# Attention outputs turned by TensorE instead of DMA transposes, the last two batches through DRAM, with feature pairs side by side

## The chip, the cores and the metric

The kernel runs on one core of a Trainium2 chip. The metric is the device time of one execution in microseconds. The time before is the median of nine runs.

## What is computed

Windowed attention over 8 batches, 8 heads, 576 positions and head size 64, then a gated network without a nonlinearity. Heads 0 to 3 look back over 32 positions, heads 4 to 7 over 128 positions in steps of four.

```python
scores = np.matmul(q, k.transpose(0, 1, 3, 2)) / np.sqrt(64)
rel = pos[:, None] - pos[None, :]
plain = (rel >= 0) & (rel < 32)                      # heads 0..3
dilated = (rel >= 0) & (rel < 128) & (rel % 4 == 0)  # heads 4..7
attn = softmax(where(mask, scores, -1e9)) @ v
x = attn.transpose(0, 2, 1, 3).reshape(4608, 512)
out = ((x @ w1) * (x @ w2)) @ w3 @ w_out
```

## The kernel before, in words

Everything is in bf16 but the inputs, the outputs and the sums. `w3 @ w_out` is formed once on the chip (`wf_sb`), so each token needs two products up (512 to 1024) and one down (1024 to 512).

*Names of the work.* A planner (`Plan`) holds a list of tasks with an engine, an assumed duration, what they depend on and a priority, lays them out in time once, when the program is built, and issues them in that order; each engine then runs its own list strictly in order. `SHIFT` adds to the priorities task by task, so it decides the order on every queue. `ON_DVE` names the PSUM copies that VectorE makes and not ScalarE. PSUM has eight banks, which the planner hands out too.

For one batch b there are two halves of heads (u = 0 plain, u = 1 dilated) and two halves of positions; the four half-steps are b.0 and b.1 (u = 0), b.2 and b.3 (u = 1). The tasks are:

- L: loads. GpSimd issues all loads that round to bf16: `load_rows` (q, k), `load_v_plain`, `load_v_dil`, `load_w` (w1 and w2, in two halves of 512 columns, LW0 and LW1), `load_wo`, `load_w3`. SP issues two f32 loads of batch 0, which ScalarE rounds. At most about eight GpSimd loads are under way; the next waits for the landing of an early one.
- T: VectorE turns q and k in blocks of 32 x 32 words of two bf16 (`turn`), so that pairs of features come to lie side by side (`qts`, `kts`); `QUARTERS` cuts some turns of batch 0 in four.
- S, E, M: scores on TensorE (L466, an operand with a step of two elements), exponentials on ScalarE (L477), masks on VectorE (L485).
- V, R, N: values on TensorE (L508, a row of ones gives the denominators), reciprocals (L519) and normalisation (L522) on VectorE into `xo`: 96 positions by 768 (three blocks of 256 features).
- The turn of `xo` to features by positions, into `XT[u]`. For batches below `TURNED` (2) it is X, six transposes on TensorE (L536), and K, the copy out of PSUM (L544 on ScalarE, L546 on VectorE). For the other six batches it is XD, one DMA transpose that SP issues (L549).
- A and B: the products up for a unit k of 288 tokens (unit k needs batch k // 2: both plain half-steps and one dilated one) and two 128-column pieces f (L573, 8 matmuls of 288 columns, 4 chunks of the contraction in `ORDER`, the dilated ones first). CA is ScalarE's copy of A (L584), G the gate on VectorE (L588) into the ring `gt`. The first `PARTED` of unit 0 are cut into a part on the plain chunks (name with p) and a part on the dilated ones.
- W3T, W3M, W3D: w3 turned on VectorE (L651), multiplied with w_out (L659), copied to `wf_sb`.
- Y, CY, ST: the product down for 128 tokens (L599, 8 matmuls of 512 columns), the copy (L609) into one of five buffers, and the stores, which SP issues (L643). The last Y is cut into two column ranges, copied by VectorE (FIN, L632).
- fill: single matmuls on zeros (L704) where TensorE would idle before the first A.

SP's list holds the stores and the DMA transposes in the planner's order: a store that is not ready holds up the transposes behind it, and the other way round. TensorE's list ends with A and B of unit 15 and Y32 to Y35.

Of the kernel before, what the change touches and what calls it, by code (L numbers as in the profile page):

```python
# [32 lines left out]
QUARTERS = ('kn',)  # L33
SINGLE = 0
TURNED = 2
# [9 lines left out]
ON_DVE = ('K0.3', 'K1.1', 'VK0.1.1', 'VK1.0.1', 'W3D2', 'W3D4', 'W3D5')  # L45
GRP = 5
WHOLE = ("qn", "kn")
B0_LOADS = ()
HELD = 4
MASK_AT = 22.5  # L50
PARTED = 4
BAND_AT = 8.2
IDENT_AT = -2.5
BUSY = 10000
LEAD = 1.2
WC = (512, 512)
SLACK = (400, 800, 2500, 5000)
# [138 lines left out]
def kernel(  # L196
# [22 lines left out]
    ctx.enter_context(tc.manual_schedule())  # L219
    plan = Plan()  # L220

    const = ctx.enter_context(tc.tile_pool(name="const", bufs=1))
    ps_pool = ctx.enter_context(tc.tile_pool(name="ps", bufs=1, space=bass.MemoryType.PSUM))
    ps = ps_pool.tile([P, 8, 512], F32, name="ps")

    w1_sb = const.tile([P, DCH, d_ff], BF16, name="w1_sb")
    w2_sb = const.tile([P, DCH, d_ff], BF16, name="w2_sb")
    wo_sb = const.tile([P, KFF, d_model], BF16, name="wo_sb")
    wf_sb = const.tile([P, KFF, d_model], BF16, name="wf_sb")
    XT = [  # L230
        const.tile([P, B * BLK, 2, QB], BF16, name="XT0"),
        const.tile([P, B * BLK, 2, QB], BF16, name="XT1"),
    ]
    gt = const.tile([P, KFF, RING], BF16, name="gt")
    ident = const.tile([P, P], BF16, name="ident")
    mask = const.tile([P, 16, QB], BF16, name="mask")
    vps = [const.tile([P, 4, 6, PITCH], BF16, name=f"vp{i}") for i in range(2)]
    vds = [const.tile([P, 4, 3, 2 * PITCH], BF16, name=f"vd{i}") for i in range(2)]
    bias = const.tile([P, 7, QB], BF16, name="bias")
    ets = [const.tile([P, 4 * GRP * QB + 32], BF16, name=f"et{i}") for i in range(4)]  # L240
    kts = [const.tile([P, 2, PADK + S, 2], BF16, name=f"kt{i}") for i in range(2)]
    qts = [const.tile([P, 2, S, 2], BF16, name=f"qt{i}") for i in range(2)]
    vts = [const.tile([P, 1, PADK + S, 2], BF16, name=f"vt{i}") for i in range(1)]
    warm = const.tile([P, 256], BF16, name="warm")
    rows_sb = {
        (nm, i): const.tile([P, n, 18 * D], BF16, name=f"{nm}{i}")
        for nm, n in (("qn", 2), ("kn", 2), ("vn", 1))
        for i in range(2)
    }
    w3ns = [const.tile([P, 8, 256], BF16, name=f"w3n{i}") for i in range(4)]  # L250
    w3Ts = [const.tile([P, 4, P, 2], BF16, name=f"w3T{i}") for i in range(3)]
    rcps = [const.tile([P, 4, 3], F32, name=f"rcp{i}") for i in range(4)]
    xos = [const.tile([P, 12 * D], BF16, name=f"xo{i}") for i in range(4)]
    asbs = [const.tile([P, 2, UNIT], BF16, name=f"asb{i}") for i in range(3)]
    osbs = [const.tile([P, d_model], F32, name=f"osb{i}") for i in range(OSB)]

    def bank(n, dtype=F32):
        at = ps[:, plan.now.place or 0, :]
        return (at if dtype == F32 else at.bitcast(dtype))[:, 0:n]

    def load_rows(nm, src, b, us):
        flat = src[b].rearrange("(u h) s d -> u (h s d)", u=2)
        flat = flat.rearrange("u (p x) -> p u x", p=P)
# [52 lines left out]
    def load_w(dst, src, f):  # L318
        nc.gpsimd.dma_start(  # L319
            out=dst[:, :, f], in_=src[:, f].rearrange("(a p) f -> p a f", p=P)  # L320
        )
# [165 lines left out]
    class Step:  # L487
# [41 lines left out]
        def cols(self):  # L529
            m0 = self.b * BLK + 3 * self.hf  # L530
            return XT[self.u][:, m0 : m0 + 3, :, :].rearrange("p m g x -> p (m g x)")

        def back(self):
            self.x = bank(6 * QB, BF16)
            for i in range(6):
                nc.tensor.transpose(  # L536
                    out=self.x[:, i * QB : (i + 1) * QB],
                    in_=self.xo[0:QB, i * P : (i + 1) * P],
                    identity=ident[0:QB, 0:QB],
                )  # L540

        def keep(self, eng):
            if eng == "ACT":
                nc.scalar.copy(out=self.cols(), in_=self.x)  # L544
            else:
                nc.vector.tensor_copy(out=self.cols(), in_=self.x)  # L546

        def back_dma(self):
            nc.sync.dma_start_transpose(  # L549
                out=self.cols().rearrange("p (i x) -> p i x", i=6),  # L550
                in_=self.xo[0:QB, :],
            )

    held = {}

    def unit_cols(k, c):

        b, hf = k // 2, k % 2  # L560
        if c < 2:
            x = XT[0][:, b * BLK : (b + 1) * BLK, c, 48 * hf : 48 * hf + 48]
            return x.rearrange("p m (r t) -> p r m t", r=2)
        return XT[1][:, 3 * k : 3 * k + 3, c - 2, :]
# [150 lines left out]
    def load(name, issue, move, deps, fn, b=0):  # L715
        dma_n[0] += 1
        return add(name, "DMA", (issue, move), [], fn, dma_n[0], lat=SLACK[min(b, 3)], after=deps)
# [28 lines left out]
    def loads_w12(c):  # L746
        return [
            load(f"LW{c}.{i}", 800, 1400 if WC[c] == 256 else 5.1 * WC[c], [],
                 lambda d=d, s=s: load_w(d, s, cols[c]))
            for i, (d, s) in enumerate(((w1_sb, moe_w1), (w2_sb, moe_w2)))  # L750
        ]
# [23 lines left out]
    for x in FIRST_LOADS:  # L775
# [6 lines left out]
        elif x[0] == "3":  # L782
            ts = [
                load(f"LW3.{c}.{g}", 550, 680, [], lambda c=c, g=g: load_w3(c, g)) for g in range(4)
            ]
            lw3[2 * c] = lw3[2 * c + 1] = ts
        elif x[0] == "d":
            loads_vd(c)
        elif x[0] == "v" and DIRECT_V <= c:
            loads_v(c)  # L790
        else:
            loads_rows(x[0] + "n", c, (int(x[2]),) if x[2:] else None)

    FUSED, w3m = [], []
    for ft in lw3:
        i = len(w3m) % 3
        x = add(f"W3T{ft}", "DVE", 1150, lw3[ft], lambda f=ft, i=i: w3_turn(f, i), RANK["W"],
                lat=80, after=w3m[-3:-2])
        z = add(f"W3M{ft}", "PE", 1728, [x, lwo[0], lwo[1]], lambda f=ft, i=i: w3_mul(f, i), 7,
                slot=1)  # L800
        w3m.append(z)
        name = f"W3D{ft}"
        eng, dur = ("DVE", 688) if name in ON_DVE else ("ACT", 585)
        FUSED.append(add(name, eng, dur, [z], lambda f=ft, e=eng: w3_done(f, e), -1, lat=100))

    kept, paced = {}, []
# [26 lines left out]
    for b in range(B):  # L833
# [71 lines left out]
        while steps < 4 * B:  # L905
            bb, i = steps // 4, steps % 4
            u, hf = i // 2, i % 2
            mine = [(bb, u, 3 * hf + mm) for mm in range(3)]
            if any(x not in grp_of for x in mine):
                break  # L910
            steps += 1
            parts = [grp_of[x][1:3] for x in mine]
            st = Step(bb, u, hf, parts)
            n = f"{bb}.{i}"
            ms = {id(t): t for x in mine for t in grp_of[x][3]}
            vv = add(f"V{n}", "PE", 390, list(ms.values()) + vals[(bb, u, hf)], st.values,
                     bb - 99 + rank("V", b), slot=2)
            for x in mine:
                readers.setdefault(grp_of[x][0], []).append(vv)
            if (bb, i) == (0, 2) and LATE:  # L920
                for t in late:
                    t.after.append(vv)
                    t.deps.append(vv)
            rc = add(f"R{n}", "DVE", 240, [vv], st.recip, 10 * bb + rank("N", bb), lat=0,
                     after=prev["x"][i])
            ns = [add(f"N{n}", "DVE", 960, [vv, rc], st.norm, 10 * bb + rank("N", bb), lat=80)]
            if bb < TURNED:
                x = add("X" + n, "PE", 270, ns + [idt], st.back, bb - 99 + rank("X", bb), slot=1)
                name = f"K{n}"
                eng, dur = ("DVE", 460) if name in ON_DVE else ("ACT", 640)  # L930
                x = [
                    add(name, eng, dur, [x], lambda st=st, e=eng: st.keep(e),
                        10 * bb + rank("K", bb), lat=100)
                ]
            else:
                x = [add("XD" + n, "SP", 1700, ns, st.back_dma, 0, lat=1200)]
            kept.setdefault(bb, []).append(x)
            prev["x"][i] = x
            vdone.setdefault((bb, u), []).append(vv)
# [114 lines left out]
```

## Time and profile before

| what | value |
|---|---|
| median of 9 runs | 249.99 us |
| lowest and highest | 248.41 and 258.92 us |
| the profiled execution | 251.70 us |
| its span | 249.8 us |
| products up, L573 | 1024 matmuls, 134.8 us busy |
| products down, L599 | 63.3 us busy |
| transposes, L536 | 48 matmuls |
| DMA transposes, L549 | 24, median 5.2 us from issue to landing, at most 16.0 |
| packets of GpSimd's queue | 39040, 62.0% of the DMA engines' time |
| packets of SP's queue | 20656, 28.2% |

Busy time of a group counts each matmul from its start to its modelled end, so overlapping ones count twice: 32 products in a row take 3.92 us, though each is listed with 286 ns. How long TensorE works on something is read from starts. In lists of instructions in order of time, a bracket gives the idle time before an instruction and what ended it. TensorE has two queues in the profile, PE for matmuls and PEld for weight loads, and a wait may show on both.

### The profile page before, as it was taken

The page shows a single profiled execution, that of the slowest core. Times are in us where ns is not written, and L with a number is a line of the kernel's source. Part 1 is how long each engine was busy: PE and PEld are TensorE (multiplying, and loading weights), DVE is VectorE, ACT ScalarE, POOL GpSimd, SP SyncE. Part 2 cuts the span into 40 slices and gives each one's busy share as a digit, 9 for nine tenths or more (in the row PEclk, how much of TensorE's full clock was granted, in tenths as well). Part 3 has the DMA queues.
Part 4 walks back from the last instruction along what each step waited for, and adds up shares of the span by engine and source line. Part 5 has one row for each costly group of instructions (what it writes and reads, how often), then busy time and mean ns, then how long its engine had stood idle before and what let it go on. Part 6 is the DMA issues. An engine that isn't in the chain of part 4 may idle for free.

```text
span 249.8 us, 6255 instructions
## 1 busy us (share of the span) xinstructions
PE 238.9 (96%) x2639; PEld 164.4 (66%) x2664; DVE 157.8 (63%) x266; ACT 107.0 (43%) x142; POOL 61.8 (25%) x94
## 2 busy tenths in 40 slices
PE   7889999989999999988999999999999999999994
PEld 5667787535675577666766767677676666777752
DVE  4878996987988977765629998267273652232221
ACT  5764633125636362524336253444344443323320
POOL 7896254584610630240100324000000000000000
PEclk9999999999999999999999999999999999999999
DMA  7999999999999999999993098822323124121114
GB/s 227 198 202 194 199 210 197 195 175 174 213 226 180 196 191 221 114 137 218 164 132 87 5 150 159 141 66 54 82 44 93 45 68 96 52 67 45 42 44 127
DMA packets 59724, 33.90 MB, mean 136 GB/s; under 512 B 44336, under 2 KB 50736, under 8 KB 59696
## 3 DMA queue, kind: packets, MB, share of 16 engines
q0 software_dynamic: 39040, 19.34, 62.0%
q1 hardware_dynamic: 20656, 14.16, 28.2%
q8 instruction: 21, 0.34, 0.6%
q14 instruction: 7, 0.06, 0.1%
HBM read 39.85 MB, written 9.44 MB: 197 GB/s over the span
## 4 chain that ended last, share of the span: by engine, by line
PE 71%; DMA 19%; POOL 4%; DVE 2%; issue 2%; DVEq 0%; POOLq 0%
PE ps L573 38%; PE ps L599 22%; DMA w3n<-in_moe_w_dram 7%; DMA w_sb<-in_moe_w_dram 5%; DMA XT<-xo 4%; PE ps L659 4%; PE ps L508 3%; PE ps L466 3%; DMA vn<-in_v_dram 3%; POOL mask L378 2%; PE ps L616 1%; POOL w_sb L319 1%; POOL vp L298 0%; POOL w3n L333 0%; DVE kt L399 0%
## 5 line engine op out<-in xcount | busy, mean ns | idle before, releaser
L573 PE MATMUL ps<-XT,w_sb 128*128 128x288 bf16 x1024 | 134.8, 286 | 1.9 <-DMA XT<-xo 1.7
L573 PEld LDWEIGHTS <-w_sb 128*128 128x128 bf16 x1024 | 97.9, 98 | 31.3 <-DMA XT<-xo 2.0
L588 DVE TENSOR_TENSOR gt<-ps,asb 128x576 bf16<-128x576 f32 x64 | 48.0, 755 | 56.1 <-PE ps L573 54.5
L584 ACT CAST asb<-ps 128x576 bf16<-128x576 f32 x64 | 40.7, 638 | 62.2 <-PE ps L573 60.1
L599 PE MATMUL ps<-wf_sb,gt 128*128 128x512 bf16 x257 | 63.3, 379 | 1.3 <-issue 0.2
L599 PEld LDWEIGHTS <-gt 128*128 128x128 bf16 x280 | 26.9, 98 | 27.5
L609 ACT COPY osb<-ps 128x512 f32<-128x512 f32 x35 | 20.4, 585 | 50.3 <-PE ps L599 49.2
L477 ACT ACTIVATE et<-ps 128x1920 bf16<-128x1920 f32 (+2 forms) x21 | 34.2, 1635 | 9.3 <-PE ps L466 9.3
L522 DVE TENSOR_TENSOR xo<-ps,rcp 96x768 bf16<-96x768 f32 x32 | 29.9, 947 | 0.7
L309 POOL DMA_DIRECT2D vd<-in_v_dram x32 | 21.4, 677 | 27.1 <-PE ps L508 24.9
L415 DVE STREAM_TRANSPOSE qt<-qn 128x320 uint32<-128x320 uint32 (+1 forms) x32 | 21.9, 703 | 2.8 <-PE ps L466 1.6
L485 DVE TENSOR_TENSOR et<-et,mask 128x960 bf16<-128x960 bf16 (+1 forms) x34 | 20.6, 643 | 1.3 <-ACT et L477 1.3
L298 POOL DMA_DIRECT2D vp<-in_v_dram x7 | 8.3, 1186 | 32.3 <-PE ps L508 20.2
L508 PEld LDWEIGHTS <-et 128*128 128x128 bf16 x384 | 14.2, 98 | 2.2 <-DMA vd<-in_v_dram 0.4
L659 PE MATMUL ps<-wo_sb,w3T 128*128 128x512 bf16 x62 | 14.2, 380 | 1.1 <-DVE w3T L651 1.0
L415 DVE STREAM_TRANSPOSE kt<-kn 128x256 uint32<-128x256 uint32 (+3 forms) x18 | 11.2, 640 | 4.3 <-PE ps L573 4.2
L466 PEld LDWEIGHTS <-kt 32*128 32x128 bf16 x768 | 9.1, 92 | 6.0 <-issue 5.3
L519 DVE RECIPROCAL rcp<-ps 96x12 f32<-96x12 f32 x32 | 6.6, 213 | 10.1 <-PE ps L508 9.9
L466 PE MATMUL ps<-qt,kt 32*128 32x96 bf16 x768 | 12.1, 201 | 0.4 <-DVE kt L399 0.4
L333 POOL DMA_DIRECT2D w3n<-in_moe_w_dram x16 | 9.3, 585 | 11.4 <-DMA wo_sb<-in_moe_w_out_dram 4.1
L659 PEld LDWEIGHTS <-w3T 128*128 128x128 bf16 x64 | 6.0, 98 | 8.7 <-DVE w3T L651 2.0
L651 DVE STREAM_TRANSPOSE w3T<-w3n 128x512 uint32<-128x512 uint32 x8 | 8.5, 1079 | 3.3 <-issue 1.8
(54 smaller groups left out, 103.2 us busy)
## 6 DMA issues: line engine op xcount, KB each, us to landing
qn<-in_q_dram POOLq DMA_DIRECT2D x6, 576.0 KB, 12.0
kn<-in_k_dram POOLq DMA_DIRECT2D x6, 576.0 KB, 12.2
w_sb<-in_moe_w_dram POOLq DMA_DIRECT2D x4, 512.0 KB, 10.3
w3n<-in_moe_w_dram POOLq DMA_DIRECT2D x16, 128.0 KB, 8.8
vp<-in_v_dram POOLq DMA_DIRECT2D x7, 288.0 KB, 9.1
out_dram<-osb SPq DMA_DIRECT2D x8, 224.0 KB, 2.4
out_dram<-osb SPq DMA_DIRECT2D x7, 256.0 KB, 3.7
out_dram<-osb SPq DMA_DIRECT2D x8, 192.0 KB, 3.5
```

Source lines behind the costliest of these rows:

```text
L309: nc.gpsimd.dma_start(out=vds[b % 2][p0 : p0 + n, :, mu, 16 : 16 + 2 * D], in_=v_rows(b, 4, 4 * t0 + res, [[4 * D, n], [S * D, 4], [1, 2 * ...
L415: nc.vector.transpose(out=o, in_=i)
L466: nc.tensor.matmul(out=self.sp[:, g, QB * i : QB * i + QB], lhsT=kt[prt, u, QB * m : QB * m + P, c], rhs=qq, start=(c == 0 and not biased) ...
L477: nc.scalar.activation(out=ev, in_=self.sp[:, :, 0:x], func=ACT.Exp, scale=scale)
L485: nc.vector.tensor_tensor(out=ev, in0=ev, in1=mk, op=AL.mult)
L508: nc.tensor.matmul(out=self.o[:, g, mm, :], lhsT=grp.et[:, c0 : c0 + P], rhs=vv, start=True, stop=True,)
L522: nc.vector.tensor_tensor(out=self.xo[0:QB, :].rearrange("p (m g d) -> p g m d", m=3, g=4), in0=self.o[0:QB, :, :, self.val : self.val + D ...
L573: nc.tensor.matmul(out=o[:, i, :], lhsT={"a": w1_sb, "b": w2_sb}[key][:, c, f * P : (f + 1) * P], rhs=unit_cols(k, c), start=(first and j ...
L584: nc.scalar.copy(out=held[("s", k, fs[0])], in_=held[("a", k, fs[0])])
L588: nc.vector.tensor_tensor(out=gt[:, fs[0] : fs[-1] + 1, c0 : c0 + UNIT], in0=held[("b", k, fs[0])], in1=held[("s", k, fs[0])], op=AL.mult,)
L599: nc.tensor.matmul(out=y, lhsT=gt[:, f, c0 : c0 + P], rhs=wf_sb[:, f, :], start=(f == 0), stop=(f == KFF - 1),)
L659: nc.tensor.matmul(out=o, lhsT=w3Ts[i][:, g // 2, :, g % 2], rhs=wo_sb[:, g, :], start=(g == 0), stop=(g == KFF - 1),)
```

## The change

Half-steps of batches 0 to 5 (`TURNED` is 6) are turned by TensorE; the DMA transposes are gone. For batches 6 and 7 there are three new tasks. F: VectorE turns `xo` in blocks of 32 x 32 words into a buffer that w3 had before. XA: SP issues three plain writes of it to DRAM, in runs of 128 bytes. UB: SP issues four reads from DRAM into `XT`, in runs of 1152 bytes, once the writes have landed. Since the turn works on words of two bf16, two neighbouring features stay side by side: `XT` is laid out with the pair innermost, the products read it with a step of two elements, TensorE's transposes read `xo` with a step of two and the copies out of PSUM write with a step of two. The rows of w1 and w2 are taken in the matching order (feature 256 u + 2 p + c), for which each of their four loads is cut into two. `QUARTERS` names q as well as k; `PARTED` is 9, so all eight products of unit 0 are cut by chunks and not four; `ON_DVE` names other copies; and all of `SHIFT` is another list, so the order on every queue is another one.

TensorE's order changes as follows where the prediction speaks of it. W3M7 comes before W3M0 and not after it. The transposes of batches 2 to 5 stand between B3.2 and B9.0; X3.1 is followed by Y10, six products with two V steps, X3.3 and X4.0, and A6.0. From A9.2 on the order is that of before. In GpSimd's list the first halves of w2 and w1 (two issues each) stand ahead of the loads of batch 1. From SP's list the transposes are gone; XA and UB of batches 6 and 7 stand among the stores ST19 to ST28, the end of it being XA7.2, ST26, UB7.2, XA7.3, ST27, UB7.3, ST28.

```diff
--- before.py
+++ after.py
@@ -30,9 +30,9 @@
 BIASED = 1
 LATE = False
 OSB = 5
-QUARTERS = ('kn',)
+QUARTERS = ('qn', 'kn')
 SINGLE = 0
-TURNED = 2
+TURNED = 6
 DIRECT_V = 1
 ORDER = (2, 3, 0, 1)
 RES = (0, 2, 1, 3)
@@ -41,14 +41,14 @@
 WARM = 25
 FILL = 110
...
-ON_DVE = ('K0.3', 'K1.1', 'VK0.1.1', 'VK1.0.1', 'W3D2', 'W3D4', 'W3D5')
...
+ON_DVE = ('K0.2', 'K1.2', 'VK0.0.1', 'VK0.1.1', 'VK1.0.0', 'VK1.0.1', 'W3D4')
 GRP = 5
 WHOLE = ("qn", "kn")
 B0_LOADS = ()
 HELD = 4
 MASK_AT = 22.5
-PARTED = 4
+PARTED = 9
 BAND_AT = 8.2
 IDENT_AT = -2.5
 BUSY = 10000
@@ -228,8 +228,8 @@
     wo_sb = const.tile([P, KFF, d_model], BF16, name="wo_sb")
     wf_sb = const.tile([P, KFF, d_model], BF16, name="wf_sb")
     XT = [
-        const.tile([P, B * BLK, 2, QB], BF16, name="XT0"),
-        const.tile([P, B * BLK, 2, QB], BF16, name="XT1"),
+        const.tile([P, B * BLK, QB, 2], BF16, name="XT0"),
+        const.tile([P, B * BLK, QB, 2], BF16, name="XT1"),
     ]
     gt = const.tile([P, KFF, RING], BF16, name="gt")
     ident = const.tile([P, P], BF16, name="ident")
@@ -251,6 +251,8 @@
     w3Ts = [const.tile([P, 4, P, 2], BF16, name=f"w3T{i}") for i in range(3)]
     rcps = [const.tile([P, 4, 3], F32, name=f"rcp{i}") for i in range(4)]
     xos = [const.tile([P, 12 * D], BF16, name=f"xo{i}") for i in range(4)]
+    dram = ctx.enter_context(tc.tile_pool(name="dram", bufs=1, space=bass.MemoryType.DRAM))
+    drs = [dram.tile([32, 12, 2 * QB], BF16, name=f"dr{i}") for i in range(4)]
     asbs = [const.tile([P, 2, UNIT], BF16, name=f"asb{i}") for i in range(3)]
     osbs = [const.tile([P, d_model], F32, name=f"osb{i}") for i in range(OSB)]
 
@@ -316,9 +318,11 @@
         nc.vector.tensor_copy(out=vp[0:32, :, 1:6, 0:D], in_=vp[96:128, :, 0:5, 0:D])
 
     def load_w(dst, src, f):
-        nc.gpsimd.dma_start(
-            out=dst[:, :, f], in_=src[:, f].rearrange("(a p) f -> p a f", p=P)
-        )
+        for u in range(2):
+            nc.gpsimd.dma_start(
+                out=dst[:, 2 * u : 2 * u + 2, f],
+                in_=src[2 * P * u : 2 * P * u + 2 * P, f].rearrange("(p c) f -> p c f", c=2),
+            )
 
     def load_wo(c):
         g = slice(4 * c, 4 * c + 4)
@@ -528,28 +532,43 @@
 
         def cols(self):
             m0 = self.b * BLK + 3 * self.hf
-            return XT[self.u][:, m0 : m0 + 3, :, :].rearrange("p m g x -> p (m g x)")
+            return XT[self.u][:, m0 : m0 + 3, :, :]
 
         def back(self):
-            self.x = bank(6 * QB, BF16)
-            for i in range(6):
-                nc.tensor.transpose(
-                    out=self.x[:, i * QB : (i + 1) * QB],
-                    in_=self.xo[0:QB, i * P : (i + 1) * P],
-                    identity=ident[0:QB, 0:QB],
+            self.x = bank(6 * QB, BF16).rearrange("p (m c x) -> p m c x", m=3, c=2)
+            xo = self.xo[0:QB, :].rearrange("p (m f c) -> p m f c", m=3, c=2)
+            for m in range(3):
+                for c in range(2):
+                    nc.tensor.transpose(
+                        out=self.x[:, m, c, :], in_=xo[:, m, :, c], identity=ident[0:QB, 0:QB]
+                    )
+
+        def keep(self, eng):
+            o = self.cols().rearrange("p m x c -> p m c x")
+            if eng == "ACT":
+                nc.scalar.copy(out=o, in_=self.x)
+            else:
+                nc.vector.tensor_copy(out=o, in_=self.x)
+
+        def flip(self):
+            self.y = w3ns[2 * self.u + self.hf].rearrange("p a x -> p (a x)")[:, 0 : 12 * D]
+            i = self.xo[0:QB, :].bitcast(U32).rearrange("p (m g f) -> p g m f", m=3, g=4)
+            o = self.y[0:QB, :].bitcast(U32).rearrange("p (g m x) -> p g m x", m=3, g=4)
+            nc.vector.transpose(out=o, in_=i)
+
+        def out_of(self):
+            self.dr = drs[2 * self.u + self.hf]
+            for a in range(3):
+                nc.sync.dma_start(
+                    out=self.dr[:, :, 64 * a : 64 * a + 64],
+                    in_=self.y[32 * a : 32 * a + 32, :].rearrange("p (q x) -> p q x", q=12),
                 )
 
-        def keep(self, eng):
-            if eng == "ACT":
-                nc.scalar.copy(out=self.cols(), in_=self.x)
-            else:
-                nc.vector.tensor_copy(out=self.cols(), in_=self.x)
-
-        def back_dma(self):
-            nc.sync.dma_start_transpose(
-                out=self.cols().rearrange("p (i x) -> p i x", i=6),
-                in_=self.xo[0:QB, :],
-            )
+        def back_in(self):
+            o = self.cols().rearrange("p m x c -> p (m x c)")
+            i = self.dr.rearrange("j (g m) x -> j g (m x)", g=4)
+            for g in range(4):
+                nc.sync.dma_start(out=o[32 * g : 32 * g + 32, :], in_=i[:, g, :])
 
 
 
@@ -559,9 +578,9 @@
 
         b, hf = k // 2, k % 2
         if c < 2:
-            x = XT[0][:, b * BLK : (b + 1) * BLK, c, 48 * hf : 48 * hf + 48]
+            x = XT[0][:, b * BLK : (b + 1) * BLK, 48 * hf : 48 * hf + 48, c]
             return x.rearrange("p m (r t) -> p r m t", r=2)
-        return XT[1][:, 3 * k : 3 * k + 3, c - 2, :]
+        return XT[1][:, 3 * k : 3 * k + 3, :, c - 2]
 
     def up(k, fs, key, chunks=ORDER, first=True, last=True):
         if first:
@@ -745,7 +764,7 @@
 
     def loads_w12(c):
         return [
-            load(f"LW{c}.{i}", 800, 1400 if WC[c] == 256 else 5.1 * WC[c], [],
+            load(f"LW{c}.{i}", 1300, 1400 if WC[c] == 256 else 5.1 * WC[c], [],
                  lambda d=d, s=s: load_w(d, s, cols[c]))
             for i, (d, s) in enumerate(((w1_sb, moe_w1), (w2_sb, moe_w2)))
         ]
@@ -791,7 +810,7 @@
         else:
             loads_rows(x[0] + "n", c, (int(x[2]),) if x[2:] else None)
 
-    FUSED, w3m = [], []
+    FUSED, w3m, w3t = [], [], {}
     for ft in lw3:
         i = len(w3m) % 3
         x = add(f"W3T{ft}", "DVE", 1150, lw3[ft], lambda f=ft, i=i: w3_turn(f, i), RANK["W"],
@@ -799,6 +818,7 @@
         z = add(f"W3M{ft}", "PE", 1728, [x, lwo[0], lwo[1]], lambda f=ft, i=i: w3_mul(f, i), 7,
                 slot=1)
         w3m.append(z)
+        w3t[ft] = x
         name = f"W3D{ft}"
         eng, dur = ("DVE", 688) if name in ON_DVE else ("ACT", 585)
         FUSED.append(add(name, eng, dur, [z], lambda f=ft, e=eng: w3_done(f, e), -1, lat=100))
@@ -933,7 +953,10 @@
                         10 * bb + rank("K", bb), lat=100)
                 ]
             else:
-                x = [add("XD" + n, "SP", 1700, ns, st.back_dma, 0, lat=1200)]
+                x = add("F" + n, "DVE", 850, ns, st.flip, 10 * bb + rank("N", bb), lat=80,
+                        after=prev["x"][i] if bb > TURNED else [w3t[2 * i], w3t[2 * i + 1]])
+                x = add("XA" + n, "SP", 1350, [x], st.out_of, 0, lat=2000)
+                x = [add("UB" + n, "SP", 3800, [x], st.back_in, 0, lat=2000)]
             kept.setdefault(bb, []).append(x)
             prev["x"][i] = x
             vdone.setdefault((bb, u), []).append(vv)
```

## The prediction

> **What bounds the kernel now.** I read the page's busy shares first, then busy time by stages, then the list of who waited for whom, then the chain that ended last, and last TensorE's instructions in order of time where that chain leaves TensorE.
>
> ```profile
> PE 238.9 (96%) x2639; PEld 164.4 (66%) x2664; DVE 157.8 (63%) x266; ACT 107.0 (43%) x142; POOL 61.8 (25%) x94
> ```
> ```profile
> 0.00:18.16 18.16, 15.23 (x241) 11.42 (x242) 12.59 (x42) 12.14 (x18) 15.69 (x29) 1.00 1.08 209
> 62.50:113.00 50.50, 48.53 (x554) 32.38 (x555) 40.42 (x66) 22.94 (x29) 14.63 (x20) 1.00 1.41 185
> 160.00:210.00 50.00, 49.58 (x588) 34.70 (x594) 26.21 (x42) 22.30 (x28) 0.00 (x0) 1.00 0.28 67
> ```
> The columns of the second view are length, busy PE, PEld, DVE, ACT and POOL, granted clock, DMA share, GB/s. TensorE is full in every stage after the first 18 us, at a granted clock of 1.00, while DMA is the crowded resource only before about 135 us. So the time is TensorE's work plus its few waits:
>
> ```profile
> PE ps L573 <- DMA XT<-xo: 1.7, 1, 1.7
> ...
> PE ps L659 <- DVE w3T L651: 1.0, 2, 0.8
> ...
> PE ps L536 <- DVE xo L522: 0.2, 1, 0.2
> PE ps L573 <- DMA w_sb<-in_moe_w_dram: 0.2, 1, 0.2
> ```
> ```profile
> 20.82 3.11 PE L573 MATMUL ps<-XT,w_sb 128*128 128x288 bf16 x24 [0.17 <-DMA w_sb<-in_moe_w_dram]
> ...
> 52.17 5.35 PE L659 MATMUL ps<-wo_sb,w3T 128*128 128x512 bf16 x24 [0.76 <-DVE w3T L651]
> ...
> 113.08 2.13 PE L573 MATMUL ps<-XT,w_sb 128*128 128x288 bf16 x16 [1.73 <-DMA XT<-xo]
> ```
> From 20.82 us to the end, the only waits of TensorE over 0.3 us are 0.76 us for the turned w3 and 1.73 us for a DMA transpose (A6.0, the first product of token unit 6, waits for XD3.2). The chain that ended last has the durations I use:
>
> ```profile
> 64.38 0.26 PE ps L536 x6
> ...
> 102.26 10.77 DMA XT<-xo
> ...
> 210.74 3.92 PE ps L573 x32
> ```
> Six transposes take 0.26 us of TensorE, 43 ns each. Thirty-two products take 3.92 us, 122.5 ns each. The late DMA transpose took 10.77 us from issue to landing, in a stage with a DMA share of 1.41.
>
> **The change, part by part.**
>
> *Sixteen half-steps (batches 2 to 5) go back to TensorE.* 16 x 0.26 = +4.16 us, in a stream that is full around all of them: all on the path. A page of the Trainium skill speaks against this harder: "TensorE: Matmul & The Clock Gate", Part 4, puts a transpose at about 275 ns in a kernel's context and says that it does not count as activity for the clock. By that page the sum would be 96 x 0.275 = 26 us. The trace has 43 ns for this very shape and no drop of the granted clock around them, so I take the trace.
>
> *Their evacuation.* 16 copies on ScalarE at 0.64 us (the row of L544, 638 to 646 ns) = 10.2 us. ScalarE is 22.9 of 50.5 us busy where most of them fall; its idle time hides them. Were that cover gone, each would delay a copy of A by 0.64 us. The copies now write every second element; the copy that already does so (L434, 768 elements, 802 ns) and the plain one (L544, 576 in 640 ns) lie on one line of 0.84 ns an element, so I add nothing. On VectorE one such copy of batch 0 (442 ns now) and one of batch 1 may lose speed, to at most 0.6 us by the same slope; +0.2 us each beside other work, nothing on the path.
>
> *The DMA transposes leave.* The 1.73 us wait goes: -1.73. Late next for A6.0 is the copy of X3.1 on ScalarE, whose transpose stands one Y (1.73 us) and six products (5.9 us) ahead of A6.0. Ends: -1.73, and 0 where that copy is late.
>
> *Waits for the new transposes.* Each stands in TensorE's fixed order behind a normalisation on VectorE (0.95 us); behind it stand products that need nothing from it, and they wait as well. Of the eight in the trace three made TensorE's two queues wait (0.8 us together), two of those in the start-up where nothing else was to do. Between 62.5 and 113 us VectorE is 80% busy. Ends: 0, and 16 x 0.4 = 6.4 us (0.4 is the longest such wait); I take +0.3, near the four of batch 1, which cost 0.2.
>
> *Start-up.* The weight loads are cut in two (four more GpSimd issues; the shortest plain load rows are 0.54 us, a whole weight load is 0.78, so up to 8 x 0.57 - 3.1 = +1.5 us on GpSimd's queue) and moved: the first halves of w2 and w1 now go ahead of the q and k loads of batch 1. The queue past them is GpSimd's: q, k and v of batch 1, then the second halves, then w3. In the trace w1's first half was issued at 5.67 and landed 8.1 us later (the shortest of the four weight loads), w2's at 11.02 with TensorE waiting to 20.82. The landings in between fit 190 to 195 GB/s of bf16 written. Counting bytes in the new order, both are there at about 17.7 us. The half-products A and B on XT0's chunks (eight instead of four) then start as soon as X0.1 is copied. Idle and fill-in matmuls between 16.86 and 20.82 are seven fills of 0.11 us and some 0.4 us of waits, 1.2 us in all: the most to gain. Ends: -1.2, and +2 if w1 (five issues further back) lands at 20 us. I take -0.6.
>
> *w3.* The program now runs W3M7 before W3M0, so the product that waited 0.76 us has 1.7 us more; as many bytes stand before its load as now. Ends: -1.0 (both waits go), and +1 from the four more issues. I take -0.76.
>
> *The last two batches.* Eight transposes on VectorE of 384 words (L415: 320 take 0.76, L399: 576 take 1.24; so 0.85 us) replace nothing on TensorE; VectorE is 26.2 of 50 us busy there. Then three writes to DRAM, a wait for their landing, and four reads, all in SP's order with stores behind them; ScalarE has five output buffers at about 6 us apart, which hides late stores. The tight place is A14.0. By the trace G12.6 ends at 206.2 and A14.0 runs at 218.2 (216.23 + 16 products). Flip to 207.1, three issues of 0.41 us (median of L643) to 208.3, landing after 1.6 to 3.8 us (stores) at 212 at the latest, four issues to 213.7, landing by 217.5: 0 us, with 0.7 us to spare at the slow end. A DMA transpose in this stretch took 2.5 to 5.2. Ends: 0, and +3 us if writing 128-byte runs is as slow as 5.2 us per leg. The skill's "DMA: Bandwidth & Descriptors", Specifications, says runs under 512 B are read, changed and written back. By that page the first leg is the slow one; no row here shows such a write.
>
> *Pairs next to each other.* The 1024 products now read their moving operand at a step of two elements. The only row with that step is the scores' (L466): 40 matmuls of 96 columns in 0.545 us, four at a time in different rows of the array, 54.5 ns per four. Half speed would be 80 ns for 96 columns, so that is out; at worst 54.5/96 = 0.57 ns a column against 0.425, which is 1024 x 288 x 0.143 ns = +42 us. At best 0. I take 0: the four start one after another, and 42.5 ns plus their offsets explains 54.5. Weights read with a step (L659) load in 98 ns like all others.
>
> **Sum.** 4.16 - 1.73 + 0.3 - 0.6 - 0.76 + 0 = +1.4 us. The profiled execution took 251.70 us (span 249.8 and 1.9 around it), so 253.1 by it. It stands 1.7 us above the median of 249.99, about what the wait for the DMA transpose cost. If the median run has that wait too, it becomes 251.4; if it has not, it becomes 253.1. The lowest run, 248.41, without that wait gives 248.41 + 3.1 = 251.5. I say **252.0**, 0.8% over the median: within what a measurement of this kernel can tell from no change, which is about 1%.
>
> **The rivals.**
> - *A14.0 waits for DRAM* (slower). Place: 207 to 218 us, SP's queue. Price: whatever the two legs take beyond 218.2; at 5.2 us a leg and 0.95 us an issue about 3 us, so 255. It decides from a landing 0.7 us later than I count. For it: the read waits behind the write's landing and a store. Against: stores land in 2.6 us at the median. Chance 0.13.
> - *TensorE waits at the new transposes* (slower). Price 16 x 0.25 = 4 us instead of 0.3: 255.7. For it: VectorE at 80%. Against: the four of batch 1 waited 0.2 us together. Chance 0.16.
> - *Start-up and w3 give all they can.* -1.2 and -1.0, no wait at a transpose: 249.99 + 4.16 - 1.73 - 2.2 = 250.2, down to 248.5 where the median run's wait was longer. To be faster by 1% the transposes would have to cost nothing as well. For it: the plain chunks of A and B can begin earlier. Against: bytes ahead of the second weight halves are the same. Chance 0.17.
> - *The step of two slows the products.* 260 to 292. Chance 0.03.
> - The forecast, 251 to 253.5: 0.51.
>
> **How the numbers follow.** The range leaves out the step's rival and the tails of the others: 249.0 (all savings) to 255.7 (one of the two waits in full). Faster by over 1% is under 247.5: 0.08, half of the third rival. Slower by over 1% is over 252.5: both slow rivals, the step's, and a fifth of the forecast, 0.42. Within 1%: 0.50.
>
> **What would show it.** Right: 144 transposes at L536's successor, 0.26 us for each six; products still at 3.92 us for 32; no TensorE wait for XT near 111 us; the turned-w3 wait below 0.3 us; the first product of A at or before 18 us; no wait ahead of A14.0. Wrong: products over 123 ns, a granted clock under 1.00, waits of the transposes for xo of over 1 us in sum, TensorE waiting for DMA into XT after 205 us, or w1 landing after 20 us.

## The result, and the profile after

The changed kernel takes 259.5 us (median of 21 runs, 258.63 to 260.51), the kernel before 250.66 us (63 runs, 248.31 to 262.64). The ratio is 1.0385, with a 95% interval of 1.0363 to 1.0408: 3.9% slower, 3.8 us above the upper end of the range. Executions of a kernel that are disturbed (those of before up to 262.64 us, and the one that was profiled of b1_mask below, in which one DMA transpose is waited for 5.86 us) are left out of the comparisons, so a ratio is not always the quotient of the two medians.

The profiled execution of after has a span of 258.0 us, against 249.8: 8.2 us to account for. The busy shares say only that TensorE is still what bounds the kernel, with 97 instructions more (96 of them the new transposes):

```profile
PE 246.5 (96%) x2736; PEld 167.1 (65%) x2762; DVE 163.9 (64%) x275; ACT 119.8 (46%) x159; POOL 64.5 (25%) x98
```

Two events cut both executions into the same three pieces: the first product of w3 with w_out, and the first Y. First before, then after; the columns are those of the stages shown ahead (length, busy PE, PEld, DVE, ACT, POOL, granted clock, DMA share, GB/s):

```profile
0.00:46.07 46.07, 42.74 (x575) 33.02 (x575) 35.76 (x77) 24.64 (x34) 29.29 (x50) 1.00 1.26 203
46.07:62.49 16.42, 15.56 (x154) 7.34 (x157) 13.36 (x18) 4.93 (x7) 10.14 (x14) 1.00 1.58 182
62.49:249.80 187.31, 180.60 (x1917) 124.07 (x1936) 108.65 (x173) 77.42 (x102) 22.32 (x30) 1.00 0.76 115
```
```profile
0.00:50.51 50.51, 44.24 (x576) 33.41 (x577) 37.87 (x80) 24.72 (x33) 34.44 (x59) 1.00 1.22 195
50.51:66.21 15.70, 15.55 (x156) 7.51 (x157) 12.37 (x16) 6.29 (x9) 7.78 (x11) 1.00 1.57 190
66.21:258.00 191.79, 186.72 (x2006) 126.22 (x2028) 113.67 (x180) 88.80 (x118) 22.26 (x30) 1.00 0.58 104
```

| stage | change |
|---|---|
| start-up, to the first w3 product | 50.51 - 46.07 = +4.44 us |
| w3 stage | 15.70 - 16.42 = -0.72 us |
| first Y to the end | 191.79 - 187.31 = +4.48 us |

The reader is to see that TensorE's idle time grew by 2.9 us in the start-up (3.3 to 6.3, the length less the busy PE) and fell by 1.6 in the last stage (6.7 to 5.1), where the extra time is busy time. These are two different losses. The first shows in TensorE's instructions of after in order of time:

```profile
16.73 0.47 PE L512 MATMUL ps<-vd,et 128*128 128x65 bf16 x10 [1.15 <-DMA vd<-in_v_dram]
...
33.83 0.20 PE L512 MATMUL ps<-vp,et 128*128 128x65 bf16 x1 [1.49 <-DVE et L489]
34.91 0.49 PE L512 MATMUL ps<-vp,et 128*128 128x65 bf16 x11 [0.87 <-DVE vp L318]
...
37.30 0.43 PE L542 MATMUL ps<-ident,xo 96*128 96x96 bf16 x6 [0.53 <-DVE xo L526]
```

These waits make 4.04 us, and none of them is for a weight. (Before has waits of its own in this piece, 0.25, 0.22, 0.17 and 0.24 us among them.) The three after 33 us have one origin. The mask multiplication L489 is VectorE's, and the same view of VectorE names what it waited for:

```profile
33.11 1.23 DVE L489 TENSOR_TENSOR et<-et,mask 128x960 bf16<-128x960 bf16 x2 [3.97 <-POOL mask L382]
34.37 0.48 DVE L318 COPY vp<-vp 32x1280 bf16<-32x1280 bf16 x1
```

VectorE stood for 3.97 us; the halo copy of `vp` (L318) and the normalisation behind it in its list came late with it. GpSimd's list of after shows why the last mask was so late:

```profile
26.16 0.71 POOL L322 DMA_DIRECT2D w_sb<-in_moe_w_dram  x1 [0.67 <-DMA qn<-in_q_dram]
...
28.19 0.59 POOL L337 DMA_DIRECT2D w3n<-in_moe_w_dram  x1 [0.71 <-DMA w_sb<-in_moe_w_dram]
29.89 0.58 POOL L337 DMA_DIRECT2D w3n<-in_moe_w_dram  x1 [1.11 <-DMA w_sb<-in_moe_w_dram]
31.64 0.70 POOL L268 DMA_DIRECT2D qn<-in_q_dram  x1 [1.18 <-ACT asb L603]
32.38 0.70 POOL L382 TENSOR_SCALAR mask<-bias 128x192 bf16<-128x192 bf16 x1
```

The mask (task masks1) needs 0.70 us of GpSimd and nothing from these loads. But it stands behind two loads of w3 and one of q, and each of those waits for an earlier load to land before GpSimd issues it. (For the q load the bracket names a copy by ScalarE, which this load does not need. The load of `vp` issued at 19.46 us took 11.6 us and landed at 31.1, just ahead of it.) In before it stood ahead of them:

```profile
21.77 0.71 POOL L378 TENSOR_SCALAR mask<-bias 128x192 bf16<-128x192 bf16 x1
```

The second loss is in the products. The last 48 products in a row, first before, then after:

```profile
233.17 6.04 PE L573 MATMUL ps<-XT,w_sb 128*128 128x288 bf16 x48
```
```profile
241.05 6.20 PE L592 MATMUL ps<-XT,w_sb 128*128 128x288 bf16 x48
```

0.16 us over 48 products is 3.3 ns each. The Y behind them, whose operands are laid out as before, did not change: 23 of their matmuls take 5.34 us in both traces. With b6's 2.6 ns a product (below) the account of the last stage reads 4.16 (transposes) - 1.73 (the wait that went) + 832 x 2.6 ns = 2.2: +4.6 against +4.48 measured. The start-up is explained less closely. Idle time grew by 2.9 us, the 192 products there make 192 x 2.6 ns = 0.5, and the 25 warm-up matmuls at its start took 5.52 us instead of 5.00; that is 3.9 of the 4.44 us. The last 0.5 us is not taken apart.

### The profile page after: what moved, and what is told of

It reads as the page before. It is cut to its first block, busy times and chain, and to the rows that moved or that the text cites. A ratio compares the mean times of both kernels' runs of the same rounds, so it can differ in the third digit from the quotient of the medians.

```text
span 258.0 us, 6508 instructions
## 1 busy us (share of the span) xinstructions
PE 246.5 (96%) x2736; PEld 167.1 (65%) x2762; DVE 163.9 (64%) x275; ACT 119.8 (46%) x159; POOL 64.5 (25%) x98
## 4 chain that ended last, share of the span: by engine, by line
PE 84%; DMA 8%; POOL 3%; issue 2%; DVE 2%; POOLq 0%; DVEq 0%
PE ps L592 46%; PE ps L618 23%; DMA w_sb<-in_moe_w_dram 8%; PE ps L678 5%; PE ps L512 4%; PE ps L470 3%; PE ps L542 2%; DVE et L489 1%; POOL vd L311 1%; PE ps L635 1%; POOL mask L382 1%; POOL w_sb L322 1%; DVE xo L526 0%; POOL qn L268 0%; POOL vn L268 0%
## 5 line engine op out<-in xcount | busy, mean ns | idle before, releaser
L592 PE MATMUL ps<-XT,w_sb 128*128 128x288 bf16 x1024 | 137.8, 286 | 0.2 <-DMA w_sb<-in_moe_w_dram 0.2
L592 PEld LDWEIGHTS <-w_sb 128*128 128x128 bf16 x1024 | 95.6, 96 | 32.9 <-DMA w_sb<-in_moe_w_dram 0.5
L489 DVE TENSOR_TENSOR et<-et,mask 128x960 bf16<-128x960 bf16 (+1 forms) x34 | 20.7, 647 | 6.4 <-POOL mask L382 4.0
L419 DVE STREAM_TRANSPOSE qt<-qn 128x320 uint32<-128x320 uint32 (+3 forms) x34 | 22.1, 673 | 3.9 <-PE ps L470 2.6
L549 ACT COPY XT<-ps 128x576 bf16<-128x576 bf16 x22 | 17.8, 810 | 12.3 <-PE ps L542 12.3
```

The costliest lines, as they stand in the source:

```text
L419: nc.vector.transpose(out=o, in_=i)
L489: nc.vector.tensor_tensor(out=ev, in0=ev, in1=mk, op=AL.mult)
L592: nc.tensor.matmul(out=o[:, i, :], lhsT={"a": w1_sb, "b": w2_sb}[key][:, c, f * P : (f + 1) * P], rhs=unit_cols(k, c), start=(first and j ...
```

## The experiments

Theory 1: the step of two in the products' moving operand costs 2 to 3 ns each, some 3 us in all. Theory 2: the start-up lost about 3 us because the last mask stands late in GpSimd's list; its rival 2a: the cut of the weight loads into eight issues is what costs, wherever the mask stands. Theory 3: the 2.5 us of gains that the prediction counted are real for every execution; its rival: they were waits of the profiled execution only. Where not said otherwise, ratios are to before, spans are those of profiled executions.

**a1_rows: pairs only where the turn by VectorE needs them.** Edit of after:

```diff
-        const.tile([P, B * BLK, QB, 2], BF16, name="XT0"),
+        const.tile([P, TURNED * BLK, 2, QB], BF16, name="XT0"),
...
+        const.tile([P, (B - TURNED) * BLK, QB, 2], BF16, name="XP0"),
```

> The changed kernel with the feature pairs side by side only for batches 6 and 7; for batches 0 to 5 the features lie in two rows as before, so the products of units 0 to 11 read with a step of one and the copies out of PSUM write with a step of one. The order on every queue is that of the changed kernel. Theory 1 (a step of two slows the products): 32 products of units 0 to 11 take 3.92 us again, those of units 12 to 15 keep 4.01; 768 x 3 ns = 2.3 us less span, about 255.7, and the copies on ScalarE fall from 0.81 to 0.64 us without an effect of their own. Rival (the 4.01 us come from something else of the new kernel, for instance its other order): no stretch of products changes, span 258.0.

Ratio 1.0335 (1.0284 to 1.0385), median 257.74 us, span 255.4. That is 2.6 us below after by the spans and 1.8 by the medians. One execution now holds both kinds of product, and that decides. TensorE in order of time (each length runs to the modelled end of the last product, so 4.08 here is 3.92 us from start to start):

```profile
132.47 4.08 PE L605 MATMUL ps<-XT,w_sb 128*128 128x288 bf16 x32
...
215.44 4.16 PE L605 MATMUL ps<-XP,w_sb 128*128 128x288 bf16 x32
```

0.08 us over 32 products is 2.5 ns each, at the same granted clock (1.00 around both). From the first Y to the end, where 576 products read XT, the time fell from 191.8 to 190.5 us: -1.3, for 576 x 2.6 ns = 1.5. Theory 1 holds. The rest of the 2.6 us is not this theory's: the wait for `vd` was 0.65 us shorter, and the start-up has a loss of its own, told at the end.

**a2_mask: after with the last mask further up.** Edit:

```diff
+    order.remove(by['masks1'])
+    order.insert(order.index(by['masks4']) + 1, by['masks1'])
```

> The changed kernel with one instruction moved: the last mask on GpSimd (192 columns) stands right after the mask of its list that came third, ahead of the loads it stood behind; nothing else moves. Theory 2 (the start-up loses its time to this mask, which stands behind loads that wait for landings): VectorE's wait of 4.0 us for the mask goes, and with it TensorE's 1.5 and 0.9 us at L512 and the 0.5 us at L542; span shorter by 2.4 to 2.9 us, about 255.4. Rival (the second weight halves and the v load of batch 1 are late as well): another wait takes the place within 1 us of it, span shorter by less than 1 us.

Ratio 1.0285 (1.0245 to 1.0325), median 256.66, span 254.9: 3.1 us below after, for moving an instruction of 0.7 us. TensorE's waits over 0.5 us, but for the fills (columns: us in total, times, longest):

```profile
PE ps L512 <- DMA vd<-in_v_dram: 1.0, 1, 1.0
PE ps L470 <- DVE kt L403: 0.6, 1, 0.6
PE ps L678 <- DVE w3T L670: 0.6, 1, 0.6
```

The waits for `et`, `vp` and `xo` are all gone, and the first w3 product starts at 46.77 instead of 50.51 us. 0.6 of the 3.7 us is given back behind it: w3's last loads are issued only 0.5 to 0.9 us earlier than in after (from 46.92 instead of 47.81 us on), so the turned w3 is late next.

**a3_whole: after with each weight load in one issue again, the mask left where it was.** The rows of w1 and w2 are then in the order of before; the products' number, shapes and steps are those of after. Edit:

```diff
     def load_w(dst, src, f):
-        for u in range(2):
-            nc.gpsimd.dma_start(
-                out=dst[:, 2 * u : 2 * u + 2, f],
...
+        nc.gpsimd.dma_start(
+            out=dst[:, :, f], in_=src[:, f].rearrange("(a p) f -> p a f", p=P)
+        )
```

> The changed kernel with each load of w1 and w2 as one issue again, in the row order of before (so the features meet other rows of the weights and the output is not the reference's); the order on every queue stays. Theory 2a (the cut of the loads delays the queue behind them): the last mask runs about 1.5 us or more earlier than 32.4, and TensorE's wait at L512 shrinks by as much; span 256 to 257. Rival 2b (its place in the list delays the mask, not the cut): the mask still runs after 31 us, span within 0.7 us of 258.0.

Ratio 1.0281 (1.0241 to 1.0322), median 256.54, span 254.9: the same 3.1 us. GpSimd in order of time:

```profile
28.51 0.71 POOL L268 DMA_DIRECT2D qn<-in_q_dram  x1 [2.48 <-DMA w_sb<-in_moe_w_dram]
29.24 0.70 POOL L380 TENSOR_SCALAR mask<-bias 128x192 bf16<-128x192 bf16 x1
```

With four issues less, the mask in the same place of the list runs at 29.24 instead of 32.38 us, and no wait for `et` is left. So in this order the cut matters as much as the place, and rival 2a cannot be put aside yet.

**b2_split: before with the weight loads cut in two, nothing else.** Edit of before, with the rows in their old order:

```diff
     def load_w(dst, src, f):
+        for u in range(2):
...
+                in_=src[2 * P * u : 2 * P * u + 2 * P, f].rearrange("(a p) f -> p a f", p=P),
```

> The kernel before with each load of w1 and w2 cut into two issues, same rows, same order on the queues. Theory 2b (the cut costs little, GpSimd's queue waits for landings anyway): within 0.7 us of before. Rival 2a (four more issues and the limit on loads under way push w3 and the masks back): 1.5 us or more, with a longer wait for the turned w3 at 52 us.

Ratio 1.0005 (0.9961 to 1.0049), span 247.6. The cut alone costs nothing: its mask still starts at 25.39 us, early enough. Rival 2a falls as a cause by itself.

**b1_mask: before with the mask late, loads whole.** One load of w3 moves with it. Edit of before:

```diff
+    order.remove(by['LW3.2.3'])
+    order.insert(order.index(by['A0.4']) + 1, by['LW3.2.3'])
+    order.remove(by['masks1'])
+    order.insert(order.index(by['LW3.2.3']) + 1, by['masks1'])
```

> The kernel before with the last mask on GpSimd moved behind the load of q of batch 2 and two loads of w3, as it stands in the changed kernel; one of these loads is issued at 31.05 us in the trace of before, so the mask would end at about 32.4 instead of 22.5. Theory 2 (the place of the mask is what the start-up lost): VectorE's first masking waits from 28.5 to 32.4 us, TensorE waits at L508 for 2 to 3 us, and the whole span grows by that, to about 252.3. Rival (the start-up of the changed kernel lost by its loads): less than 1 us.

Ratio 1.024 (1.0181 to 1.0299), median 255.6. The mask now starts at 31.56 us. The place alone, pushed this far, costs before 2.4%, about 6 us: more than expected. The wait at the V steps is there (TensorE's waits), and the stage behind it shows what came on top; the long wait for a DMA transpose in this execution lies at 121 us, far behind both:

```profile
PE ps L508 <- DVE et L485: 3.0, 2, 2.7
```
```profile
34.00:37.70 3.70, 3.70 (x28) 2.61 (x27) 2.91 (x6) 0.64 (x1) 1.73 (x4) 0.55 1.23 208
```

After the wait TensorE ran 3.7 us at a granted clock of 0.55, which costs 3.7 x 0.45 = 1.7 us more. In this execution the first w3 product starts 4.6 us late: 3.0 + 1.7. What the remaining 1 to 2 us of the ratio are is open.

So theory 2 holds in this form: cut and place together make the mask late, and undoing either of them gives the 3.1 us back.

**a4_twice: after with the transposes of batches 2 to 5 done twice.** Edit:

```diff
-            for m in range(3):
+            for m in 2 * (0, 1, 2) if self.b >= 2 else range(3):
```

> The changed kernel with the transposes of batches 2 to 5 done twice by TensorE, 96 matmuls more, the same output. Theory (each six cost 0.26 us of a full stream): 16 x 0.26 = 4.2 us more, span 262.2. Rival (they sit in idle time of TensorE, and the loss is elsewhere): less than 1 us more.

Ratio 1.0571 (1.0526 to 1.0616), median 263.77, span 262.1: +4.1 us over after, for 96 more transposes at 43 ns (4.13). All of them lie on the path.

**b3_w3, b4_x32, b5_both: before with the counted gains alone.** b3 swaps W3M7 and W3M0 (with their turns and copies). b4 turns half-step 3.2, the one that made A6.0 wait, by TensorE after Y9 and drops XD3.2; b5 does both.

```diff
+    for x, y in (("W3T0", "W3T7"), ("W3M0", "W3M7"), ("W3D0", "W3D7")):
+        i, j = order.index(by[x]), order.index(by[y])
+        order[i], order[j] = order[j], order[i]
...
+    x = Task("X3.2", "PE", 0, [], st.back, 0, 1, 0, ())
+    order.insert(at, x)
...
+    order.remove(by["XD3.2"])
```

> The kernel before with W3M7 ahead of W3M0 (and the turns and copies that belong to them swapped), as in the changed kernel; nothing else. Theory: the wait of 0.76 us for the turned w3 goes, 0.5 to 0.8 us less. Rival: the load of the next piece lands late as well, no gain.

> The kernel before with one of its 24 DMA transposes (half-step 3.2, the one that TensorE waited 1.73 us for) done by TensorE, six matmuls after Y9, and copied by ScalarE. Theory: 0.26 us more work and 1.73 us less wait, 1.0 to 1.5 us less in the profile. Rival (another transpose is late in its place, or the wait is there only in some executions): less than 0.5 us.

> The kernel before with W3M7 ahead of W3M0 and half-step 3.2 turned by TensorE, the two parts of the new order that removed waits. Theory: no wait for the turned w3 and none for the DMA transpose of 3.2; 0 to 0.4% less than before, since most executions of before have neither wait in full. Rival: another transpose becomes late and takes the gain back.

Ratios 0.997 (0.9919 to 1.0022), 1.0012 (0.9967 to 1.0056) and 0.9976 (0.9938 to 1.0014). In b3's profile the wait for w3T is gone, in b4's and b5's the wait for XT; the time does not follow. Nor is it shown that the edits removed them. b2, which keeps the order of w3 and the DMA transpose of 3.2, has neither wait in its profile: TensorE runs without a gap through the w3 products, and through A6.0, the second 16 of these 32:

```profile
46.58 10.54 PE L661 MATMUL ps<-wo_sb,w3T 128*128 128x512 bf16 x48
...
108.82 4.08 PE L575 MATMUL ps<-XT,w_sb 128*128 128x288 bf16 x32
```

b4 has one in the start-up instead, where its edit changes nothing:

```profile
PE ps L573 <- ACT asb L584: 0.7, 1, 0.7
```

So of the 2.5 us that two waits of one profiled execution promised, at most 0.6% (1.5 us) can be in a comparable execution of before, and nothing is shown. How long TensorE waits for the DMA transpose of 3.2 differs from profile to profile: not at all in b2 and b3, 1.2 us in b6, 1.7 in before, 5.9 in b1. All 18 executions of b4 and b5, which turn 3.2 by TensorE, lie between 248.54 and 250.76 us, those of before on the same two chips between 248.21 and 258.80. That suggests that this one transpose spreads them; it is not shown. No kernel tried here beats before measurably.

**b6_step: before with products that read every second element.** The buffer is filled as before and read with the step. Edit of before:

```diff
+        x = XT[1][:, 3 * k : 3 * k + 3, :, :].rearrange("p m g x -> p m (g x)")
+        return x[:, :, c - 2 : 192 : 2]
```

> The kernel before with the products reading every second element of the same two-row buffer (so they mix features and positions, and the output is not the reference's); all else as before. Theory 1: 32 products take 4.0 us instead of 3.92, 1024 x 3 ns = 3 us more, 1.2% over before on the same chip. Rival: the products stay at 3.92 us, and the slower ones of the changed kernel come from where its buffers lie.

Ratio 1.0111 (0.99 to 1.0322): by itself no verdict. The profile has one. TensorE in b6, then in b5, where the same products read without a step:

```profile
36.96 9.17 PE L575 MATMUL ps<-XT,w_sb 128*128 128x288 bf16 x72
```
```profile
37.65 8.98 PE L573 MATMUL ps<-XT,w_sb 128*128 128x288 bf16 x72
```

0.19 us over 72 products: 2.6 ns each, and the last 48 take 6.20 us, as in after. Theory 1 holds without anything else of the change.

**a5_all: after with a1, a2, and the fourth load of `vd` (LD0.3) ahead of the weights.** Edit besides those two:

```diff
+    order.remove(by['LD0.3'])
+    order.insert(order.index(by['LD0.2']) + 1, by['LD0.3'])
```

> The changed kernel with three things undone at once: features in two rows for batches 0 to 5, the last mask moved up, and one load of dilated v of batch 0 (LD0.3) put ahead of the first half of w2, where TensorE waited 1.2 us for it. Theory (the loss is transposes 4.2 us, step of two 3 us, mask 3 us, this load 1 us): what is left over the kernel before is the 16 transposes and the step in batches 6 and 7; span about 251.4, time about 253.2, 2% over the kernel before on the same chip. Rival (the new order of SHIFT costs something that no wait shows): span over 253.5.

Ratio 1.0187 (1.0104 to 1.0271), median 254.86, span 252.9. The first A starts at 17.97 us instead of 19.00 and the wait for `vd` is gone, so that wait was the place of LD0.3. But two others are there (TensorE's waits):

```profile
PE ps L691 <- DVE w3T L683: 0.6, 1, 0.6
PE ps L605 <- DMA w_sb<-in_moe_w_dram: 0.5, 1, 0.5
```

5.1 of the 8.2 us are won back, not 6.6. What is left over the profiled before is 3.1 us: 4.16 for the transposes - 1.73 for the wait that went, and 0.7 for the 256 products on XP (256 x 2.6 ns). Against comparable executions of before the ratio makes it 4.7 us (2.6 to 6.8), near 4.16 + 0.7 without that wait.

## Why the prediction was wrong, step by step

*Sixteen half-steps, +4.16.* Right: 144 transposes, 0.26 us for six, all on the path (a4: +4.1 for as many again). The clock stayed at 1.00 around them.

*Their evacuation.* Nothing on the path, right; the price of a copy was wrong. The groups of before and after by form:

```profile
L544 ACT COPY XT<-ps 128x576 bf16<-128x576 bf16 x6 | 3.7, 641 | 1.9 <-PE ps L536 1.9
```
```profile
L549 ACT COPY XT<-ps 128x576 bf16<-128x576 bf16 x22 | 17.8, 810 | 12.3 <-PE ps L542 12.3
L551 DVE COPY XT<-ps 128x576 bf16<-128x576 bf16 x2 | 1.6, 804 | 0.1
```

Writing every second element took ScalarE 810 ns instead of 641 and VectorE 804 instead of 442 (at most 600 had been said). "I add nothing" rested on a slope through L434, a copy of another size; two sizes cannot separate a cost of the layout from one of the length. ScalarE, 46% busy, hid it.

*Waits for the new transposes, +0.3.* Slightly too much: none of the sixteen waited. The one wait of 0.53 us is at a transpose of batch 1, in the start-up, and went with the late mask (a2). The rival of 4 us did not come.

*The last two batches, 0.* Right. A14.0 waited for nothing: the writes landed in 2.1 us at the median (3.9 at most), the turn took 0.57 us and not 0.85. Only the issue of a write was dearer, 0.62 us and not 0.41. ScalarE waited 2.8 us once for a store behind the reads, which TensorE did not notice.

*Start-up, -0.6.* This is the step that failed most: +4.44 instead of -0.6. It says "the queue past them is GpSimd's: q, k and v of batch 1, then the second halves, then w3", and then counts bytes until the weights land. The weights came in time (TensorE waits for w_sb once, 0.15 us, its weight queue 0.5), but the first A ran at 19.00 us and not by 18. What the step left out of the queue was what was not a weight: one load of `vd`, 1.15 us (a5; the wait is 0.5 to 1.5 us in a1 to a4, which leave this load where it was), and the last mask, 3.1 us (a2, a3, b1, b2). Its count of issues, +1.5 us on GpSimd, was right in kind; it was asked only when weights land, and not which compute instruction waits in the same list.

*w3, -0.76.* The wait went (stage -0.72). In b3 the same edit gives nothing measurable, and b2 has no such wait without it.

*Pairs next to each other, "At best 0. I take 0".* The second step that failed: 2.5 to 3.3 ns a product, about 3 us over 1024, so that its own sign of being wrong, products over 123 ns, came true. The row that spoke for a cost was there (four matmuls of 96 columns at a step of two in 54.5 ns), and was explained away by an assumed offset; between 0 and 42 us the best end was taken. A cost of 2% on 125 us is as large as all the other terms but one, so "0" needed a row as exact as 1%, and there was none. The Trainium skill, "SBUF — State Buffer", in the note on cachelines under "Door 1: The DMA port swizzle", would have backed the 0: it counts strides of up to 8 bf16 elements as free. Here a step of 2 was nearly free, 125.1 ns against 122.5, and the measurement decides.

*The sum's base.* -1.73 and -0.76 were taken off the profiled execution and then, in part, off the median. b3, b4 and b5 show that a comparable execution of before has at most 1.5 us of them to give, and b2's profile has neither. The prediction said "If the median run has that wait too", and went between; by the runs the case without it was the right one.

In the prediction's terms: 4.16 (transposes) - 1.73 - 0.72 (waits that went) + 2.9 (idle time of the start-up) + 1024 x 2.6 ns = 2.7 makes 7.3 us, and with the 0.5 of the warm-up matmuls 7.8, against 8.2 between the two profiled executions; 0.4 us stays open.

## What to carry to other kernels

When loads are cut or moved in an in-order queue, list every instruction of that queue that is not a load, and find who waits for it: here 0.7 us of mask work behind loads cost 3 us, and either of two small edits gave it back. A layout change that touches the bounding engine's every instruction is not worth 0 until a row shows it to better than its share of the span. A wait seen in one profiled execution is a gain only if the median has it: look for it in a second profile, or make the edit that removes it alone, before it enters a sum.

## What the runs showed of the hardware

Short waits of TensorE can cost more than their length. In a1_rows two waits with one matmul between them were followed by products at nearly half speed; TensorE in order of time, and the stage around it:

```profile
32.38 0.20 PE L516 MATMUL ps<-vp,et 128*128 128x65 bf16 x1 [1.59 <-DVE et L493]
33.46 0.76 PE L516 MATMUL ps<-vp,et 128*128 128x65 bf16 x11 [0.88 <-DVE vp L322]
34.04 2.11 PE L605 MATMUL ps<-XT,w_sb 128*128 128x288 bf16 x8
```
```profile
32.00:36.00 4.00, 2.74 (x21) 1.91 (x22) 3.69 (x7) 0.00 (x0) 3.70 (x7) 0.61 1.27 204
```

Eight products took 2.11 us there and 1.15 a little later. The profiled execution of after has nearly the same two waits (1.49 and 0.87) and a clock of 1.00 throughout, so a1's gain is hidden in part by this. Other executions of after seem to have such a stretch: in 8 of 22 the mean granted clock is 0.993 or lower, which is what 1.7 us lost of 258 makes, and in all eight of a2 and a3, where the mask is early, it is 0.999 or 1.00. The Trainium skill, "TensorE: Matmul & The Clock Gate", Part 1, "What's actually happening", describes a clock that falls to half after at least one idle window of about 3.4 us. The half speed agrees (a granted clock of 0.50 from 34 to 37 us in b1 and from 33 to 36 us in a1), the length doesn't: waits of 2.7 us, and of 1.6 and 0.9 with a matmul between, were enough.

Writes to DRAM in runs of 128 bytes and their reading back, bounded at up to 5.2 us a leg ahead, landed in 2.1 and 1.8 us at the median in a stretch with a DMA share of 0.38 (174 to 226 us).
